# Attention and two MoEs on one core: the first MoE's weight conversions are cut into four parts, one place apart, and held in order

## The chip, the cores and the metric

The kernel runs on one core of a Trainium2 chip. The metric is the device time of one execution in microseconds, the median of three runs. Every time of an engine below comes from one profiled execution of the kernel before.

## The reference

All inputs are stored in 64 bits. The kernel works in 32-bit arithmetic on a high and a low part of each number, so a product of two numbers is three matmuls (high·high, high·low, low·high).

```
scores = q @ k^T / sqrt(64) + decay of log f, causal          (4 batches, 8 heads, 576 positions, 64 dims)
x  = softmax(scores) @ v                                      -> 2304 tokens x 512
h  = max(x @ w1, x @ w2, x @ w3)                              w1, w2, w3: 512 x 768
x2 = h @ w_out                                                w_out: 768 x 512
h2 = x2 @ w_in                                                w_in: 512 x 2048
g  = (a0 + a1 h2 + a2 h2^2 + a3 h2^3) / (1 + |b0| |h2| + |b1| h2^2 + 1e-6)
out = g @ moe2_w_out                                          moe2_w_out: 2048 x 512
```

## The kernel before

Attention is worked off in 20 pairs of heads (`pairs`), numbered 0 to 19. The first eight are batch 0, four for query group 0 and four for group 1 ("pair 8" is the first of batch 1). Tile names carry the numbers: `s3_0_8_1_1` is a bank of scores of pair 8, `e4_7_1_1` an exponential of pair 7, `tp`/`pt` the transposed exponentials, `o` the attention output, `x` its copy that the first MoE reads. TensorE also runs warm-up products (L84) at the start.

The first MoE takes 6 chunks of 128 hidden columns: `moe1_h(b, g, fc, j)` makes product j of chunk fc (tile `h0`, `h1` or `h2`; the running maximum is `m1`, `m2`), `moe1_o(b, g, dc)` the output `x2p`, copied to `xo`. These pieces of work are taken from a queue (`units`) and put between the attention's, six times per attention step (`fill`), so they fill TensorE while the attention waits. The output `x2p` needs all six chunks of `w_out` (`wo_0` to `wo_5`, each converted in two halves).

Weights come as 64-bit numbers and are converted on the chip in four parts (`stages`): the magnitude on ACT (L179, tile `cv_...`), four operations on its bits on DVE (L184, L185, L186, L189), the high part on ACT (L195), the low part by a subtraction on POOL (L198). The first MoE has 18 conversions of 128x512 (`cv_w0_0` to `cv_w2_5`, w1 to w3 of chunk 0 to 5) and 12 of 128x256 (`cv_wo_0_0` to `cv_wo_5_1`). `cv` tiles share six buffers with four live x tiles, so two conversions are under way at once: a magnitude waits for the low part of the conversion two before it. In `fill`, a conversion is one entry of the list `conv`: all four parts are issued in one place, with the load of the weights two conversions ahead in front (`pipelined`).

A scheduler puts the instructions of each engine into one static order, in which the engine then runs; a row waits for its inputs and everything behind it on that engine waits too. An instruction that is held (`keep_in_program_order`, here also `pinned`) stays behind the instruction of its engine that the program issued just before it; others are placed by the scheduler. Before, the conversions' parts are not held, and neither are the two operations on the gate's coefficients `ab` (L674 on DVE, L675 on ACT).

Of the kernel before, what the change touches and what calls it, by code (L numbers as in the profile page):

```python
# [11 lines left out]
AF = mybir.ActivationFunctionType  # L12
ALU = mybir.AluOpType
# [24 lines left out]
def kernel(  # L38
    ctx: ExitStack, tc: tile.TileContext, q, k, v, f, w1, w2, w3, w_out, m2_in, m2_out, m2_a, m2_b, out
):  # L40
    nc = tc.nc
# [6 lines left out]
    NF1 = FF1 // P  # L48
# [4 lines left out]
    def r32(ap):  # L53
        return ap.bitcast(F32)
# [7 lines left out]
    mpool = ctx.enter_context(tc.tile_pool(name="mpool", bufs=1, side="left"))  # L62
# [57 lines left out]
    LOOK, WHOLE, PRE = 2, 6, 2  # L120
# [33 lines left out]
    w1t, wot = {}, {}  # L154
# [6 lines left out]
    def load_raw(src, nm_):  # L161
        shape = list(src.shape)
        rp, rt, rb = (mpool, "x1", 8) if shape[1] * shape[2] <= 256 else (wpool, "x2", 6)
        raws[nm_] = rp.tile(shape[:-1] + [2 * shape[-1]], I32, name=f"raw_{nm_}", tag=rt, bufs=rb)
        tc.keep_in_program_order(nc.sync.dma_start(raws[nm_], src.bitcast(I32)))

    def stages(split, src, nm_, pool, tag, bufs, pin):
        shape = list(src.shape)
        at = {}

        def held(ins):
            return tc.keep_in_program_order(ins) if pin else ins

        def magnitude():
            raw = raws.pop(nm_)
            raw = raw.rearrange("p c (f t) -> p c f t", t=2)
            at["low"], at["top"] = raw[:, :, :, 0], raw[:, :, :, 1]
            at["t"] = pool.tile(shape, I32, name=f"cv_{nm_}", tag=tag, bufs=bufs)
            held(nc.scalar.activation(at["t"].bitcast(F32), at["top"].bitcast(F32), AF.Abs))  # L179

        def bits():
            t, low, top = at["t"], at["low"], at["top"]
            tf = t.bitcast(F32)
            held(nc.vector.tensor_scalar(tf, tf, E_LO, E_HI, op0=ALU.max, op1=ALU.min))  # L184
            nc.vector.tensor_scalar(t, t, 0x07FFFFFF, 3, op0=ALU.bitwise_and, op1=ALU.logical_shift_left)  # L185
            nc.vector.scalar_tensor_tensor(  # L186
                out=t, in0=low, scalar=29, in1=t, op0=ALU.logical_shift_right, op1=ALU.bitwise_or
            )
            nc.vector.scalar_tensor_tensor(  # L189
                out=t, in0=top, scalar=-0x40000000, in1=t, op0=ALU.bitwise_and, op1=ALU.bitwise_or  # L190
            )

        def high():
            at["hi"], at["lo"] = split()
            held(nc.scalar.activation(at["hi"], at["t"].bitcast(F32), AF.Copy))  # L195

        def low():
            held(nc.gpsimd.tensor_tensor(at["lo"], at["t"].bitcast(F32), r32(at["hi"]), op=ALU.subtract))  # L198

        return [magnitude, bits, high, low]  # L200

    def convert(hi, lo, src, nm_, pool, tag, bufs):
        for f_ in stages(lambda: (hi, lo), src, nm_, pool, tag, bufs, False):
            f_()

    def rows(w):
        return w.rearrange("(c p) f -> p c f", p=P)

    def raw_w1(fc, j):
        return rows((w1, w2, w3)[j])[:, :, fc * P : (fc + 1) * P], f"w{j}_{fc}"  # L210

    def convert_w1(fc, j):
        if fc not in w1t:
            w1t[fc] = [wpool.tile([P, 3, NDC, P], F32R, name=f"w1{x}_{fc}", tag="w", bufs=12) for x in "hl"]
        hi, lo = (t[:, j] for t in w1t[fc])
        convert(hi, lo, *raw_w1(fc, j), mpool, "x0", 6)

    def raw_wo(fc, z):
        return rows(w_out)[:, fc : fc + 1, z * 256 : (z + 1) * 256], f"wo_{fc}_{z}"

    def convert_wo(fc, z):
        if fc not in wot:
            wot[fc] = wpool.tile([P, 2, DM], F32R, name=f"wo_{fc}", tag="x2", bufs=6)
        hi, lo = (wot[fc][:, x : x + 1, z * 256 : (z + 1) * 256] for x in range(2))
        convert(hi, lo, *raw_wo(fc, z), mpool, "x0", 6)

    wpd = dram.tile([P, NF2, 2, DM], F32R, name="wpd")

# [18 lines left out]
    def pipelined(work, look):  # L247

        n = len(work)

        def go(i):
            for j in range(0 if i == 0 else i + look, min(i + look + 1, n)):
                work[j][0]()
            work[i][1]()

        return [lambda i=i: go(i) for i in range(n)]
# [5 lines left out]
    def pinned(ld):  # L262
        tc.keep_in_program_order(ld)
# [234 lines left out]
    def moe1_units(b, g):  # L498
# [7 lines left out]
    pairs = [Pair(n, *j) for n, j in enumerate(jobs)]  # L506
    slots = [Unit(p, h, g) for p in pairs for g in p.groups for h in range(2)]
    first = {u.pair.n: i for i, u in reversed(list(enumerate(slots)))}
    conv = [
        (lambda fc=fc, j=j: load_raw(*raw_w1(fc, j)), lambda fc=fc, j=j: convert_w1(fc, j))  # L510
        for fc in range(NF1)
        for j in range(3)
    ]
    conv += [
        (lambda fc=fc, z=z: load_raw(*raw_wo(fc, z)), lambda fc=fc, z=z: convert_wo(fc, z))
        for fc in range(NF1)
        for z in range(2)
    ]
    conv = pipelined(conv, LOOK)
    wps = [(c, z) for c in range(NF2) for z in range(2)]  # L520
    conv2 = []
    for i, cz in enumerate(wps):
# [19 lines left out]
    state = {"m": 0, "of": 1, "n": 0}  # L542
    queue = []

    def fill(step):

        want = conv_due(step)
        while conv and len(conv) > want:
            conv.pop(0)()
        if step >= CONV2[0] and conv2:  # L550
            state["c2"] += 4 * CONV2[1]
            while conv2 and state["c2"] >= 1:
                state["c2"] -= 1
                conv2.pop(0)()
        state["m"] += 1
        while units and (state["n"] - len(units)) * state["of"] < state["n"] * state["m"]:
            units.pop(0)()
        if not units and queue and queue[0][0] in ends:
            at, new = queue.pop(0)
            units.extend(new)  # L560
            state["of"] = max(1, NFILL * (ends[at] - step) - 3)
            state["n"], state["m"] = len(units), 0
# [2 lines left out]
    state["c"] = state["c2"] = 0.0  # L565

    def conv_due(step):
        state["c"] += 0.15 if step < 7 else 0.5
        return NCONV - int(state["c"])

    pairs[0].load()
# [8 lines left out]
    ab = const.tile([P, 8], F32, name="ab")  # L580
    pinned(nc.sync.dma_start(ab[:, 0:4], m2_a.partition_broadcast(P)))
    pinned(nc.sync.dma_start(ab[:, 4:6], m2_b.partition_broadcast(P)))
    for step in range(len(slots) + 2):
        u = slots[step] if step < len(slots) else None
        t = slots[step - 1] if 0 <= step - 1 < len(slots) else None
# [85 lines left out]
        for x in range(2):  # L671
            pinned(move(wpt[n][x][:, : c1 - c0], wpd[:, c0:c1, x]))

    nc.vector.tensor_scalar(ab[:, 0:4], ab[:, 0:4], -1.0, None, op0=ALU.mult)  # L674
    nc.scalar.activation(ab[:, 6:7], ab[:, 5:6], AF.Abs)  # L675
    nc.vector.memset(ab[:, 7:8], 1.0 + 1.0e-6)
    a0, a1, a2, a3, b0, _, b1, one = (ab[:, i : i + 1] for i in range(8))

# [160 lines left out]
```

## Time and profile before

| | |
|---|---|
| median of 3 runs | 963.07 us (962.58 to 964.19) |
| the profiled execution's own time | 963.76 us |
| its span on the core | 961.9 us, mean TensorE clock 0.991 |
| TensorE (PE) busy | 936.5 us, 97% |
| VectorE (DVE) busy | 728.7 us, 76% |
| ScalarE (ACT) busy | 642.7 us, 67% |
| GpSimd (POOL) busy | 254.7 us, 26% |

"Busy" counts a matmul from its issue to its modelled end, so PE shows as busy in a stretch in which it could do more; the number of its instructions in a window tells how much it did. [...]

### The profile page before, as it was taken

How to read it: one execution, taken by the hardware profiler on the slowest of the kernel's cores; microseconds unless marked ns; L12 is line 12 of the kernel's file. 1: busy time of each engine (PE TensorE's matmuls, PEld its weight loads, DVE VectorE, ACT ScalarE, POOL GpSimd, SP SyncE). 2: the span in 40 equal slices, each digit the busy share in tenths (PEclk: the TensorE clock that was granted, in tenths of full speed). 3: DMA queues.
4: the chain of work that ended last, by engine and by line, in shares of the span. 5: the costliest groups of instructions: out<-in, count | busy, mean ns of one | idle time of the engine just before them, and what ended most of it. 6: DMA issues, size and time to landing. Idle time of an engine off the chain costs nothing.

```text
span 961.9 us, 16831 instructions
## 1 busy us (share of the span) xinstructions
PE 936.5 (97%) x5780; PEld 828.1 (86%) x5780; DVE 728.7 (76%) x1689; ACT 642.7 (67%) x1526; POOL 254.7 (26%) x408
## 2 busy tenths in 40 slices
PE   7989989999999999999999999999999999999998
PEld 6758879997998999999999988888888888999997
DVE  4688985555776776535287969888988988899997
ACT  5886666777776777657444557667766766677765
POOL 2647664444553644524223400000000000000000
PEclk9988999999999999999999999999999999999999
DMA  5685323223455465230045567011002102100000
GB/s 154 165 241 142 81 56 102 54 55 106 130 144 186 134 176 154 70 100 7 27 151 175 165 238 287 1 45 44 1 1 66 44 1 64 46 1 1 33 1 33
DMA packets 125621, 88.52 MB, mean 92 GB/s; under 512 B 74448, under 2 KB 110304, under 8 KB 125536
## 3 DMA queue, kind: packets, MB, share of 16 engines
q1 hardware_dynamic: 125536, 87.45, 30.5%
q8 instruction: 46, 0.75, 0.3%
q14 instruction: 39, 0.32, 0.1%
HBM read 64.73 MB, written 22.69 MB: 91 GB/s over the span
## 4 chain that ended last, share of the span: by engine, by line
PE 79%; DVE 11%; ACT 4%; DMA 3%; issue 2%; POOL 0%; SPq 0%; DVEq 0%; ACTq 0%; POOLq 0%
PE hq L714 7%; PE hq L712 7%; PE oo L762 7%; PE hq L713 7%; PE oo L763 7%; PE oo L761 7%; PE h L465 5%; PE h L466 5%; PE h L467 5%; PE o L433 5%; PE tp L417 4%; PE s L380 2%; PE s L381 2%; PE x2p L490 2%; PE x2p L492 2%
## 5 line engine op out<-in xcount | busy, mean ns | idle before, releaser
L465 PE MATMUL h<-x,w1h 128*128 128x320 f32 (+1 forms) x576 | 176.9, 307 | 1.7 <-DVE x L441 1.1
L466 PE MATMUL h<-x,w1h 128*128 128x320 f32 (+1 forms) x576 | 172.8, 300 | 0.0
L467 PE MATMUL h<-x,w1l 128*128 128x320 f32 (+1 forms) x576 | 172.3, 300 | 0.0
L397 POOL TENSOR_SCALAR e<-e,rs 128x64 f32<-128x64 f32 (+4 forms) x160 | 89.4, 574 | 105.6 <-DVE rs L394 90.9
L388 ACT ACTIVATE e<-e,st 128x64 f32<-128x64 f32 (+4 forms) x160 | 89.1, 558 | 41.1 <-DVE st L382 39.8
L465 PEld LDWEIGHTS h<-x,w1h 128*128 128x128 f32 x576 | 109.8, 191 | 5.1 <-DVE x L441 2.0
L762 PE MATMUL oo<-wp,gh 128*128 128x512 f32 x288 | 112.6, 391 | 0.0
L761 PE MATMUL oo<-wp,gh 128*128 128x512 f32 x288 | 112.0, 389 | 0.0
L466 PEld LDWEIGHTS h<-x,w1h 128*128 128x128 f32 x576 | 110.0, 191 | 0.6 <-issue 0.5
L467 PEld LDWEIGHTS h<-x,w1l 128*128 128x128 f32 x576 | 109.8, 191 | 0.1
L721 ACT ACTIVATE s<-hq 128x512 f32<-128x512 f32 (+1 forms) x80 | 44.3, 554 | 97.7 <-PE hq L714 97.7
L763 PE MATMUL oo<-wp,gl 128*128 128x512 f32 x288 | 109.1, 391 | 0.0
L382 DVE CUSTOM_DVE_ANT_0 e<-s,mask 128x320 f32<-128x320 f32 (+3 forms) x160 | 67.6, 431 | 36.8 <-PE s L381 21.6
L419 ACT ACTIVATE pt<-tp 128x384 f32<-128x384 f32 (+3 forms) x160 | 69.6, 468 | 18.5 <-PE tp L417 15.6
L417 PE MATMUL tp<-ident,e 128*128 128x128 f32 (+1 forms) x480 | 77.9, 279 | 2.8 <-DVE k2s L310 1.7
L724 DVE SCALAR_TENSOR_TENSOR s<-s,ab,u 128x512 f32<-128x512 f32 (+1 forms) x80 | 55.7, 696 | 32.3 <-ACT u L722 32.1
L714 PE MATMUL hq<-x,wil 128*128 128x512 f32 (+1 forms) x192 | 69.9, 364 | 0.0
L712 PE MATMUL hq<-x,wih 128*128 128x512 f32 (+1 forms) x192 | 69.8, 363 | 0.0
L713 PE MATMUL hq<-x,wih 128*128 128x512 f32 (+1 forms) x192 | 69.7, 363 | 0.0
L763 PEld LDWEIGHTS oo<-wp,gl 128*128 128x128 f32 x288 | 54.1, 188 | 11.4
L761 PEld LDWEIGHTS oo<-wp,gh 128*128 128x128 f32 x288 | 54.1, 188 | 10.5
L417 PEld LDWEIGHTS tp<-ident,e 128*128 128x128 f32 (+1 forms) x480 | 55.8, 134 | 8.5 <-POOL e L397 2.7
(131 smaller groups left out, 2429.6 us busy)
## 6 DMA issues: line engine op xcount, KB each, us to landing
raw_w<-in_moe_w_dram SPq DMA_DIRECT2D x18, 512.0 KB
raw_wp<-in_moe_w_out_dram SPq DMA_DIRECT2D x32, 256.0 KB
wpd<-wp SPq DMA_DIRECT2D x32, 256.0 KB
raw_wi<-in_moe_w_in_dram SPq DMA_DIRECT2D x32, 256.0 KB
wp<-wpd SPq DMA_DIRECT2D x10, 768.0 KB
x2d<-xo SPq DMA_DIRECT2D x16, 320.0 KB
out_dram<-ob SPq DMA_DIRECT2D x18, 256.0 KB
kn<-in_k_dram SPq DMA_DIRECT2D x32, 128.0 KB
```

Of the source, the lines that this page charges most:

```text
L388: nc.scalar.activation(e[:nr], e[:nr], AF.Exp, bias=m, scale=-1.0, accum_out=l)
L397: nc.gpsimd.tensor_scalar(e, e, self.rs[:, 1, j : j + 1], 0.0, op0=ALU.mult, op1=ALU.add)
L417: nc.tensor.transpose(tp[:kr, dst : dst + P], self.e[i][:, Q0[c] : Q1[c]], ident)
L465: nc.tensor.matmul(hp_[:, :w], wh[:, j, dc], xs[dc][:, 1], start=(dc == NDC - 1), stop=False)
L466: nc.tensor.matmul(hp_[:, :w], wh[:, j, dc], xs[dc][:, 0], start=False, stop=False)
L467: nc.tensor.matmul(hp_[:, :w], wl[:, j, dc], xs[dc][:, 0], start=False, stop=(dc == 0))
L712: nc.tensor.matmul(hp_[:, :w], wih[:, dc, fs], xh, start=(dc == 0), stop=False)
L713: nc.tensor.matmul(hp_[:, :w], wih[:, dc, fs], xl, start=False, stop=False)
L714: nc.tensor.matmul(hp_[:, :w], wil[:, dc, fs], xh, start=False, stop=(dc == NDC - 1))
L761: nc.tensor.matmul(o, g[0][:, ts_], wh_, start=(fc == 0), stop=False)
L762: nc.tensor.matmul(o, g[0][:, ts_], wl_, start=False, stop=False)
L763: nc.tensor.matmul(o, g[1][:, ts_], wh_, start=False, stop=(fc == NF2 - 1))
```

## The change

Each of the 30 conversions becomes two entries of `conv`, an even and an odd place. Even place k loads the weights two ahead, issues the high part of conversion k−1 and then the magnitude of conversion k. Odd place k issues the low part of conversion k−1 and then the bits of conversion k. All of these are held on their engine (of the four DVE operations the first). The pace doubles, since there are twice as many entries: as many conversions per step as before, each ending one place later. L674 and L675 are held too, which keeps them behind the instructions issued before them at the end of the attention.

```diff
-    conv = [
-        (lambda fc=fc, j=j: load_raw(*raw_w1(fc, j)), lambda fc=fc, j=j: convert_w1(fc, j))
...
-    conv = pipelined(conv, LOOK)
+    firsts = [(raw_w1(fc, j), lambda fc=fc, j=j: split_w1(fc, j)) for fc in range(NF1) for j in range(3)]
+    firsts += [(raw_wo(fc, z), lambda fc=fc, z=z: split_wo(fc, z)) for fc in range(NF1) for z in range(2)]
+    parts1 = [stages(split, *raw, mpool, "x0", 6, True) for raw, split in firsts]
+
+    def part1(i, *which):
+        if 0 <= i < len(parts1):
+            for x in which:
+                parts1[i][x]()
+
+    def even(k):
+        for raw, _ in firsts[0 if k == 0 else k + LOOK : k + LOOK + 1]:
+            load_raw(*raw)
+        part1(k - 1, 2)
+        part1(k, 0)
+
+    def odd(k):
+        part1(k - 1, 3)
+        part1(k, 1)
+
+    conv = []
+    for i in range(len(firsts) + 1):
+        conv += [lambda i=i: even(i), lambda i=i: odd(i)]
...
-        state["c"] += 0.15 if step < 7 else 0.5
+        state["c"] += 0.3 if step < 7 else 1.0
...
-    nc.vector.tensor_scalar(ab[:, 0:4], ab[:, 0:4], -1.0, None, op0=ALU.mult)
-    nc.scalar.activation(ab[:, 6:7], ab[:, 5:6], AF.Abs)
+    pinned(nc.vector.tensor_scalar(ab[:, 0:4], ab[:, 0:4], -1.0, None, op0=ALU.mult))
+    pinned(nc.scalar.activation(ab[:, 6:7], ab[:, 5:6], AF.Abs))
```

The change adds and removes no instruction of an engine that computes; it moves them. Line numbers from about L210 on differ between the two kernels: from the pairs to the first MoE's products those of the changed kernel are lower by two (L382 there reads L380, L490 reads L488). The text uses those of the kernel before.

On DVE, around the conversion of chunk 4 (the number at the end of a name counts tiles), the order before is:

```order
L184 TENSOR_SCALAR cv_w0_4_861<-cv_w0_4_861 128x512
L185 TENSOR_SCALAR cv_w0_4_861<-cv_w0_4_861 128x512
L186 SCALAR_TENSOR_TENSOR cv_w0_4_861<-raw_w0_4_795,cv_w0_4_861 128x512
L184 TENSOR_SCALAR cv_w1_4_902<-cv_w1_4_902 128x512
L189 SCALAR_TENSOR_TENSOR cv_w0_4_861<-raw_w0_4_795,cv_w0_4_861 128x512
L394 RECIPROCAL rs_5_1_1_1116<-rs_5_1_1_1116 128x2
L185 TENSOR_SCALAR cv_w1_4_902<-cv_w1_4_902 128x512
L186 SCALAR_TENSOR_TENSOR cv_w1_4_902<-raw_w1_4_818,cv_w1_4_902 128x512
```

and in the changed kernel:

```order
L184 TENSOR_SCALAR cv_w0_4_852<-cv_w0_4_852 128x512
L185 TENSOR_SCALAR cv_w0_4_852<-cv_w0_4_852 128x512
L186 SCALAR_TENSOR_TENSOR cv_w0_4_852<-raw_w0_4_771,cv_w0_4_852 128x512
L189 SCALAR_TENSOR_TENSOR cv_w0_4_852<-raw_w0_4_771,cv_w0_4_852 128x512
L439 TENSOR_TENSOR x_4_1_1_1044<-o_4_1_1_1033,x_4_1_1_1044 128x256
L184 TENSOR_SCALAR cv_w1_4_894<-cv_w1_4_894 128x512
L185 TENSOR_SCALAR cv_w1_4_894<-cv_w1_4_894 128x512
```

Two conversions were woven into each other; now the four rows of one stand together, and the next conversion's first follows its last with one other row between.

On ACT, at the same conversions, the order before is:

```order
L179 ACTIVATE cv_w0_4_861<-raw_w0_4_795 128x512
L135 ACTIVATE q2s01_1635<-mask_92,unit_99 2x320
L388 ACTIVATE e4_5_1_1_1132,rs_5_1_1_1116<-e4_5_1_1_1132,st_5_1_1_1115 128x576
L179 ACTIVATE cv_w1_4_902<-raw_w1_4_818 128x512
L393 ACTIVATE rs_5_1_1_1116<-rs_5_1_1_1116,tiny_97 128x2
L470 ACTIVATE m0_0_0_0_882<-h0_0_0_0_869 128x320
L195 ACTIVATE w1h_4_859<-cv_w0_4_861 128x512
```

and in the changed kernel:

```order
L179 ACTIVATE cv_w0_4_852<-raw_w0_4_771 128x512
L417 ACTIVATE pt1_128<-tp0_5_0_1_1067 128x512
L438 ACTIVATE x_4_1_1_1044<-o_4_1_1_1033 128x256
L417 ACTIVATE pt1_128<-tp1_5_0_1_1078 128x384
L195 ACTIVATE w1h_4_891<-cv_w0_4_852 128x512
L179 ACTIVATE cv_w1_4_894<-raw_w1_4_811 128x512
```

The magnitude of `w1_4` stood ahead of the high part of `w0_4`; now it stands right behind it.

On DVE, at the end of the conversions, the order before is:

```order
L189 SCALAR_TENSOR_TENSOR cv_wo_5_0_1496<-raw_wo_5_0_1417,cv_wo_5_0_1496 128x256
L189 SCALAR_TENSOR_TENSOR cv_wo_5_1_1514<-raw_wo_5_1_1450,cv_wo_5_1_1514 128x256
L382 ISA e4_7_1_1_1599,st_7_1_1_1591<-s4_1_7_1_1_1604,mask_92,st_7_1_1_1591 128x256
L382 ISA st_7_1_1_1591 128x1
L394 RECIPROCAL rs_7_1_1_1592<-rs_7_1_1_1592 128x2
L495 TENSOR_TENSOR xo_0_0_0_2072<-x2p_0_0_0_2053,xo_0_0_0_2072 128x320
```

and in the changed kernel:

```order
L380 ISA e4_8_0_1_1859,st_8_0_1_1851<-s4_1_8_0_1_1864,mask_92,st_8_0_1_1851 128x256
L380 ISA st_8_0_1_1851 128x1
L184 TENSOR_SCALAR cv_wo_5_1_1513<-cv_wo_5_1_1513 128x256
L185 TENSOR_SCALAR cv_wo_5_1_1513<-cv_wo_5_1_1513 128x256
L380 ISA e3_8_1_1_1942,st_8_1_1_1940<-s3_0_8_1_1_1943,mask_92 128x448
L380 ISA st_8_1_1_1940 128x1
L186 SCALAR_TENSOR_TENSOR cv_wo_5_1_1513<-raw_wo_5_1_1441,cv_wo_5_1_1513 128x256
...
L189 SCALAR_TENSOR_TENSOR cv_wo_5_1_1513<-raw_wo_5_1_1441,cv_wo_5_1_1513 128x256
```

Before, the last conversion and `xo_0_0_0` behind it stand among the rows of pair 7. In the changed kernel both stand among those of pair 8: 25 rows, nearly all of pair 8's attention, are ahead of `xo_0_0_0` that were behind it (12 scores rows at L382, each with its small read-out row, 5 at L310, 4 at L322, 3 reciprocals and an x). Ahead of that, the scores come earlier among the conversions: the four bits operations of 20 conversions stood ahead of pair 6's last scores row on DVE, and 16 do now. PE's order answers to it: 53 matmuls of pair 8's attention stand ahead of the first product with `wo_5` that stood behind it, 71 ahead of `x2p_0_0_2`; at `h0_1_0_0` (batch 1's first product) less than ten are left of that, and the second MoE's rows on PE are in the same order in both kernels. L674 and L675 stand just ahead of the second MoE's first gate instead of at the 13th microsecond.

## Rows read from the trace of the kernel before

**Rows 1.** The page, chain that ended last, shares of the span.

```profile
PE 79%; DVE 11%; ACT 4%; DMA 3%; issue 2%; POOL 0%; SPq 0%; DVEq 0%; ACTq 0%; POOLq 0%
```

**Rows 2.** Windows (us, busy us of each engine (instructions), TensorE clock, DMA share, GB/s).

```profile
10.00:20.00 10.00, 9.06 (x49) 7.06 (x48) 2.48 (x17) 6.18 (x22) 1.24 (x4) 1.00 0.47 114
70.00:80.00 10.00, 8.74 (x27) 6.16 (x27) 9.89 (x21) 7.47 (x18) 7.91 (x7) 0.50 0.61 194
160.00:170.00 10.00, 10.00 (x88) 9.27 (x85) 6.66 (x21) 7.11 (x19) 7.47 (x14) 1.00 0.30 68
220.00:230.00 10.00, 8.54 (x65) 5.90 (x64) 5.77 (x23) 8.32 (x27) 4.07 (x9) 1.00 0.59 168
```

**Rows 3.** The same view, one window over the conversions' stretch.

```profile
52.00:142.00 90.00, 80.19 (x483) 65.84 (x480) 80.95 (x182) 61.33 (x152) 53.47 (x61) 0.91 0.47 130
```

**Rows 4.** The same window, instructions on tile cv_w alone.

```profile
52.00:142.00 90.00, 36.03 (x48) 14.97 (x24) 17.81 (x12) 0.91 0.47 130
```

**Rows 5.** The same window, instructions on tile cv_wo alone.

```profile
52.00:142.00 90.00, 23.44 (x48) 10.00 (x24) 9.70 (x12) 0.91 0.47 130
```

**Rows 6.** Line L184, 10 to 52 us (ns min/median/max).

```profile
L184 DVE TENSOR_SCALAR cv_w<-cv_w x6: 406/424/428, 22.5 to 40.1; 128x512 f32<-128x512 f32 x6
```

**Rows 7.** Line L186, 10 to 52 us.

```profile
L186 DVE SCALAR_TENSOR_TENSOR cv_w<-raw_w,cv_w x6: 676/690/932, 23.4 to 42.6; 128x512 int32<-128x512 int32 x6
```

**Rows 8.** Line L184, 52 to 142 us.

```profile
L184 DVE TENSOR_SCALAR cv_wo<-cv_wo x12: 278/291/1006, 103.6 to 132.1; 128x256 f32<-128x256 f32 x12
```

**Rows 9.** Line L186, 52 to 142 us.

```profile
L186 DVE SCALAR_TENSOR_TENSOR cv_wo<-raw_wo,cv_wo x12: 407/517/1445, 104.5 to 135.9; 128x256 int32<-128x256 int32 x12
```

**Rows 10.** Line L198, 52 to 142 us.

```profile
L198 POOL TENSOR_TENSOR w1l<-cv_w,w1h x12: 1273/1447/1716, 59.7 to 104.4; 128x512 fp32r<-128x512 f32 x12
L198 POOL TENSOR_TENSOR wo<-cv_wo,wo x12: 731/814/957, 108.8 to 139.2; 128x256 fp32r<-128x256 f32 x12
```

**Rows 11.** Groups by line and form, 52:142: busy us, mean ns | idle before, releaser.

```profile
L179 ACT ACTIVATE cv_w<-raw_w 128x512 f32<-128x512 f32 x12 | 7.9, 667 | 3.4 <-DMA raw_w<-in_moe_w_dram 2.2 <-POOL w1l L198 1.2
...
L195 ACT ACTIVATE w1h<-cv_w 128x512 fp32r<-128x512 f32 x12 | 7.5, 627 | 6.1 <-DVE cv_w L189 6.1
L184 DVE TENSOR_SCALAR cv_w<-cv_w 128x512 f32<-128x512 f32 x12 | 7.4, 617 | 2.5 <-ACT cv_w L179 2.3
...
L179 ACT ACTIVATE cv_wo<-raw_wo 128x256 f32<-128x256 f32 x12 | 5.1, 436 | 1.5 <-POOL wo L198 0.8 <-POOL w1l L198 0.6
L195 ACT ACTIVATE wo<-cv_wo 128x256 fp32r<-128x256 f32 x12 | 5.0, 414 | 5.1 <-DVE cv_wo L189 4.9
L382 DVE CUSTOM_DVE_ANT_0 e<-s,mask 128x448 f32<-128x448 f32 x8 | 4.9, 616 | 0.1
...
L184 DVE TENSOR_SCALAR cv_wo<-cv_wo 128x256 f32<-128x256 f32 x12 | 4.7, 395 | 1.3 <-ACT cv_wo L179 1.2
```

**Rows 12.** Timeline of DVE (start us, us).

```profile
64.73 0.85 DVE L185 TENSOR_SCALAR cv_w<-cv_w 128x512 int32<-128x512 int32 x1
65.62 1.64 DVE L186 SCALAR_TENSOR_TENSOR cv_w<-raw_w,cv_w 128x512 int32<-128x512 int32 x1
67.18 0.41 DVE L184 TENSOR_SCALAR cv_w<-cv_w 128x512 f32<-128x512 f32 x1
```

**Rows 13.** Timeline of POOL, the same stretch.

```profile
65.27 1.44 POOL L198 TENSOR_TENSOR w1l<-cv_w,w1h 128x512 fp32r<-128x512 f32 x1
```

**Rows 14.** Timeline of POOL, ACT and DVE at one hand-over.

```profile
82.97 2.97 POOL L198 TENSOR_TENSOR w1l<-cv_w,w1h 128x512 fp32r<-128x512 f32 x2
83.58 0.63 ACT L195 ACTIVATE w1h<-cv_w 128x512 fp32r<-128x512 f32 x1 [1.97 <-DVE cv_w L189]
...
84.71 0.67 ACT L179 ACTIVATE cv_w<-raw_w 128x512 f32<-128x512 f32 x1 [0.51 <-POOL w1l L198]
...
85.41 0.81 DVE L184 TENSOR_SCALAR cv_w<-cv_w 128x512 f32<-128x512 f32 x1 [1.87 <-ACT cv_w L179]
```

**Rows 15.** The chain from 10 to 24 us (start us, us, what).

```profile
12.61 3.40 DMA ab<-in_moe_b_dram
```

More of the change, by code (lines that the diff above doesn't have):

```diff
@@ L210, in raw_w1, with split_w1, split_wo @@
         return rows((w1, w2, w3)[j])[:, :, fc * P : (fc + 1) * P], f"w{j}_{fc}"
-    def convert_w1(fc, j):
+    def split_w1(fc, j):
         if fc not in w1t:
             w1t[fc] = [wpool.tile([P, 3, NDC, P], F32R, name=f"w1{x}_{fc}", tag="w", bufs=12) for x in "hl"]
-        hi, lo = (t[:, j] for t in w1t[fc])
-        convert(hi, lo, *raw_w1(fc, j), mpool, "x0", 6)
+        return [t[:, j] for t in w1t[fc]]
     def raw_wo(fc, z):
         return rows(w_out)[:, fc : fc + 1, z * 256 : (z + 1) * 256], f"wo_{fc}_{z}"
-    def convert_wo(fc, z):
+    def split_wo(fc, z):
         if fc not in wot:
             wot[fc] = wpool.tile([P, 2, DM], F32R, name=f"wo_{fc}", tag="x2", bufs=6)
-        hi, lo = (wot[fc][:, x : x + 1, z * 256 : (z + 1) * 256] for x in range(2))
-        convert(hi, lo, *raw_wo(fc, z), mpool, "x0", 6)
+        return [wot[fc][:, x : x + 1, z * 256 : (z + 1) * 256] for x in range(2)]
     wpd = dram.tile([P, NF2, 2, DM], F32R, name="wpd")
@@ L508 @@
     first = {u.pair.n: i for i, u in reversed(list(enumerate(slots)))}
-    conv = [
-        (lambda fc=fc, j=j: load_raw(*raw_w1(fc, j)), lambda fc=fc, j=j: convert_w1(fc, j))
[L511 to L518, printed above, removed]
-    conv = pipelined(conv, LOOK)
+    firsts = [(raw_w1(fc, j), lambda fc=fc, j=j: split_w1(fc, j)) for fc in range(NF1) for j in range(3)]
[16 more added lines that the diff above has]
+        conv += [lambda i=i: even(i), lambda i=i: odd(i)]
     wps = [(c, z) for c in range(NF2) for z in range(2)]
```

## The prediction

> **What bounds the kernel now.** The chain that ended last comes first: 79% of the span is TensorE (PE) and 11% VectorE (DVE) [rows 1]. The windows say where the DVE part lies. In 160:170 PE issues 88 matmuls in 10 us, 0.114 us each, and is full [rows 2]. In 52:142, where 24 of the first MoE's 30 conversions run, it issues only 483 in 90 us, while DVE is busy 80.95 of the 90 [rows 3]. So here DVE sets the pace and PE waits for what it makes. Two windows of the tiles show what DVE does: 36.03 us on `cv_w` (48 operations, 12 conversions, 3.00 us each) and 23.44 on `cv_wo` (1.95 each) [rows 4, 5]. Behind this stretch PE is nearly always full, so what is lost in it stays lost; the one hole after it that concerns us is 220:230, with 65 matmuls [rows 2].
>
> **DVE's price for a conversion is not its own.** Undisturbed, L184 takes 0.424 us and L186 0.690 [rows 6, 7], and L185 and L189 go like these; a `cv_w` conversion is then 2 × (0.424 + 0.690) = 2.23 us. For `cv_wo` I take 0.29 and, as the shortest of its scan operations, 0.41 [rows 8, 9], so 1.40. Over the window that is 12 × 2.23 + 12 × 1.40 = 43.6 us against 59.5 measured: 15.9 us are stretching. The timeline shows the cause: L186 at 65.62 takes 1.64 us, to 67.26 [rows 12], and POOL's low part ran from 65.27 to 66.71 [rows 13]. The DVE operation ends 0.55 us after the low part does. It did not run slower beside it, it hardly ran.
>
> **The change, part by part,** against the profiled execution's 963.76 us, which is 0.7 above the median.
>
> (a) Order of the work. 25 rows of DVE work, mostly pair 8's, now lie ahead of the first MoE's output. By the forms' means in the stretch (0.616 us for the largest L382 [rows 11], a reciprocal about 0.16) I estimate 10.2 us, and 9.5 when neighbours overlap as at 67.18, which starts 0.08 before the row ahead of it ends [rows 12]. Against it PE gets 71 matmuls to do ahead of `x2p_0_0_2`: 71 × 0.114 = 8.1 us. What PE loses by waiting longer for the last conversion, it does meanwhile: +9.5 − 8.1 = **+1.4**. Bounds: −8.1, if DVE is not what PE waits for there, and +9.5, if PE waited elsewhere for lack of the work moved.
>
> (b) Hand-over waits. Since ACT runs in order and the magnitude of k now stands behind the high part of k−1, DVE's L184 of k waits after L189 of k−1 for L195 and L179: 0.627 + 0.667 = 1.29 us for `cv_w`, 0.414 + 0.436 = 0.85 for `cv_wo` [rows 11], less the rows that stand between on DVE. The order has 24 such places in the stretch. In two of the twelve of `cv_w` nothing stands between, in nine a row or a few short ones, in one enough: I get 10.5 us of waits. For `cv_wo` four have nothing between, four some, four enough: 5.0 us. Before, DVE waited there 2.5 + 1.3 = 3.8 us [rows 11]. So 15.5 − 3.8 = **+11.7**. The trace shows the hand-over once: L195 at 83.58, L179 at 84.71 (0.51 of it waiting for a low part), L184 at 85.41, with DVE idle 1.87 us [rows 14]. Bounds: 0, if DVE is not the bound at these places; 24 × 1.3 = 31 as the trace's worst kind.
>
> (c) Less stretching. The low part of k−1 can start when its high part is done, beside the magnitude of k, so it now runs in the wait. It takes at least 1.273 us for `cv_w` and 0.731 for `cv_wo` [rows 10], the magnitude 0.667 and 0.436, so it outlasts the wait by 0.61 or 0.30 us. L184 would be caught in this rest, as at 85.41, where it took 0.81 us and the low parts ended at 85.94 (82.97 + 2.97) [rows 14]. So the 15.9 us of stretching fall to about 11 × 0.6 + 9 × 0.3 = 9.3: **−6.6**. Bounds: −15.9, if L184 runs freely beside a low part, and 0.
>
> [...]
>
> (d) Dependent neighbours. The four bits operations now stand in a row, and each needs the one before: L186 at 65.62 starts 0.04 after L185's end, where independent rows overlap by 0.08 [rows 12]. Some 15 more such pairs at 0.12: **+1.8**.
>
> (e) ACT's own work. The high part is needed at once now, but waits behind whatever stands ahead of it on ACT, which is busy 61.33 of the 90 us [rows 3]. 20 places at 0.08: **+1.5** (0 to +5). Behind it, magnitude, L184 and so DVE are late too.
>
> (f) The ab operations. L675 leaves the start, where its DMA stands in the chain with 3.40 us [rows 15]. But PE is busy 9.06 of 10 us in 10:20, with its warm-up products [rows 2], so it gains only its holes: **−1.0** (0 to −2.8). At the new place, the DMA is long done and PE full: nothing, hidden by the products queued there.
>
> (g) Loads. Loading raw weights earlier takes away ACT's wait for `raw_w`, 2.2 us in the stretch [rows 11]. Half of it I count: **−1.2** (0 to −2.2). The loads now stand ahead of kn_2 on the DMA queue; PE has its warm-up products to cover a late kn_2, without which it would cost what three loads take.
>
> (h) The hole in 220:230. There the first MoE's pieces have run out; now they come some 8 us later and fill it: (88 − 65) × 0.114 = 2.6 us missing, of which I take **−2.0** (0 to −2.6).
>
> Parts that only change place in the second MoE have the same order on PE and cost nothing, since PE is full there.
>
> Sum: 1.4 + 11.7 − 6.6 + 1.8 + 1.5 − 1.0 − 1.2 − 2.0 = +5.6. One correction: DVE's other waits in the stretch. It is idle 90 − 80.95 = 9.05 us, of which 3.8 are counted in (b). The other 5.2 are for PE and ACT, and partly vanish when DVE runs late: **−2.2** (0 to −5). That leaves +3.4: 967.2 for the profiled execution, **966.5** for the median.
>
> **Rivals.** [...]
>
> *Faster, about 957.* The waits of (b) fall where PE has attention work: 16 conversions stand ahead of pair 6's last scores on DVE where 20 did, four of some 3 us or less each, so PE is fed some 10 us earlier from 70:80 on, where it is poorest. Then (b) costs only half, 5.8, and the sum is 3.4 − 5.9 = −2.5; with (c) at −11 it is −6.9, thus 956.2. It decides when half of the hand-overs lie behind a PE that has work. For it: 27 matmuls in 70:80 leave much to win. Against it: DVE is at 9.89 of 10 there [rows 2], and it has the 9.5 us of (a) more to do before `x2p` can go on.
>
> *No change, 963.* Everything in the stretch is an exchange: (b) and (c) cancel, PE's work ahead covers (a), and the pieces that are late come even by batch 1. It needs (b) to be 3 us less, well within its bounds.
>
> **How the numbers follow.** What a measurement of this kernel tells from no change is about 0.2%, 1.9 us. The forecast case (964.9 to 969) has 0.35, the slower rival 0.18, no change 0.20, faster 0.27: together faster 0.27, same 0.20, slower 0.53. The range runs from 957, at the faster rival, to 973, the slower one and a little of what (e) can still add; what lies outside has about 2 in 10.
>
> **What would show it.** After the change, DVE's idle time before L184 in the first MoE's stretch should be near 15 us and be released by L179, against 3.8; L186 and L189 should come down to near 0.69 us, and L184 go up; a `cv_w` conversion should fall from 3.00 us on DVE to about 2.8. `xo_0_0_0` should come some 10 us later than before, the scores of pair 8 earlier. L675 should no longer stop ACT near 13 us, and 220:230 should hold over 80 matmuls. The prediction is wrong if those waits are there but PE's matmuls in 52:142 do not fall, or if the order of the loads makes a new wait for kn_2 or for a raw weight.

## The result, and the profile after

The changed kernel takes 969.71 us in the median (967.89 to 973.23, 5 runs) against 963.07 before (also 5 runs); the ratio is 1.0075 with a 95% interval of 1.0063 to 1.0087. The change makes the kernel slower by about 7 us. The runs spread over 5 us where those of before spread over 1.6; the longest also has the lowest mean TensorE clock (0.977, against 0.983 to 0.985 in the other four). The profiled execution is the shortest of the five: 967.89 us, 4.1 above that of before.

On the page of the changed kernel, DVE has a smaller share of the chain that ended last (8% for 11%) and PE a larger one:

```profile
PE 84%; DVE 8%; ACT 4%; issue 2%; DMA 1%; SPq 0%; POOL 0%; DVEq 0%; ACTq 0%; POOLq 0%
```

This row alone would mislead. PE's share also holds matmuls at a granted clock of 0.50 (19 in 75:85). The windows of the changed kernel show where the time went (columns as in [rows 2]):

```profile
10.00:20.00 10.00, 9.80 (x54) 7.81 (x52) 3.97 (x20) 7.34 (x25) 1.68 (x4) 1.00 0.63 183
70.00:80.00 10.00, 4.95 (x19) 2.91 (x17) 7.94 (x16) 6.02 (x15) 5.42 (x6) 0.67 0.30 92
80.00:90.00 10.00, 7.15 (x39) 5.28 (x40) 6.44 (x11) 5.53 (x12) 3.00 (x3) 0.62 0.58 188
140.00:150.00 10.00, 5.97 (x29) 4.82 (x29) 8.13 (x23) 7.08 (x21) 7.34 (x12) 0.78 0.18 46
220.00:230.00 10.00, 10.00 (x86) 9.02 (x86) 3.38 (x13) 5.69 (x20) 3.15 (x7) 1.00 0.14 34
...
52.00:142.00 90.00, 74.07 (x449) 60.79 (x447) 72.74 (x159) 54.66 (x137) 44.65 (x53) 0.89 0.47 131
```

In 52:142 PE issues 449 matmuls, 34 fewer than before, and DVE is busy 8 us less [rows 3]: DVE did not become faster, it waits. Two poor stretches stand out, 70:90 and 140:150. The hole in 220:230 has closed (86 matmuls for 65 [rows 2]) and 10:20 holds 54 for 49.

What DVE waits for is one line. The waits of DVE in 52:162 of the changed kernel (us in total, times, longest), and below them the same two of the kernel before:

```profile
DVE cv_w L184 <- ACT cv_w L179: 11.1, 11, 1.4
DVE cv_wo L184 <- ACT cv_wo L179: 4.3, 7, 0.8
...
DVE cv_w L184 <- ACT cv_w L179: 2.3, 2, 1.9
DVE cv_wo L184 <- ACT cv_wo L179: 1.2, 2, 0.9
```

15.4 us against 3.5 before. The waits of PE in the same stretch show who pays. The x of L439 (L441 before) and the maximum m of L470 (L472 before) stand on DVE behind conversions; POOL's L395 (L397 before) follows a reciprocal on DVE. The changed kernel, and below it the two of these waits that the kernel before has:

```profile
PE tp L415 <- POOL e L395: 6.9, 3, 2.6
PE o L431 <- DVE x L439: 5.0, 1, 5.0
PE h L463 <- DVE m L470: 2.8, 2, 2.3
...
PE h L465 <- DVE m L472: 0.7, 2, 0.4
PE tp L417 <- POOL e L397: 0.6, 1, 0.6
```

One hand-over, in the timelines of DVE, ACT and POOL of the changed kernel:

```profile
56.75 0.69 DVE L189 SCALAR_TENSOR_TENSOR cv_w<-raw_w,cv_w 128x512 int32<-128x512 int32 x1
...
58.70 1.04 DVE L184 TENSOR_SCALAR cv_w<-cv_w 128x512 f32<-128x512 f32 x1 [0.86 <-ACT cv_w L179]
...
57.47 0.63 ACT L195 ACTIVATE w1h<-cv_w 128x512 fp32r<-128x512 f32 x1 [0.48 <-DVE cv_w L189]
58.01 0.66 ACT L179 ACTIVATE cv_w<-raw_w 128x512 f32<-128x512 f32 x1
...
58.18 1.27 POOL L198 TENSOR_TENSOR w1l<-cv_w,w1h 128x512 fp32r<-128x512 f32 x1 [3.65 <-ACT w1h L195]
```

L189 ends at 57.44. Then come the high part, the magnitude, and only at 58.70 the next L184; a scores row on DVE covers some of the wait, 0.86 us is idle. The low part runs from 58.18 to 59.45, and L184, undisturbed 0.42 us long, ends at 59.74, 0.29 us after it.

The groups of the conversions in 52:162 of the changed kernel (busy us, mean ns | idle before, releaser):

```profile
L184 DVE TENSOR_SCALAR cv_w<-cv_w 128x512 f32<-128x512 f32 x12 | 11.7, 975 | 11.1 <-ACT cv_w L179 11.1
L186 DVE SCALAR_TENSOR_TENSOR cv_w<-raw_w,cv_w 128x512 int32<-128x512 int32 x12 | 9.3, 779 | 0.2
L189 DVE SCALAR_TENSOR_TENSOR cv_w<-raw_w,cv_w 128x512 int32<-128x512 int32 x12 | 9.0, 754 | 0.2
...
L185 DVE TENSOR_SCALAR cv_w<-cv_w 128x512 int32<-128x512 int32 x12 | 7.9, 658 | 0.2
L184 DVE TENSOR_SCALAR cv_wo<-cv_wo 128x256 f32<-128x256 f32 x12 | 7.6, 637 | 4.3 <-ACT cv_wo L179 4.3
```

Last, when the same matmul starts in both profiled executions (the static order of PE set against the trace; us):

```
                                  before   after
first of h0_0_0_0                  76.86   86.88   +10.0
last scores bank of pair 7        132.73  139.29    +6.6
x2p_0_0_2                         142.33  164.06   +21.7
last scores bank of pair 8        160.95  161.60    +0.7
h0_1_0_0, where the orders meet   231.09  239.30    +8.2
last scores bank of pair 15       353.07  358.73    +5.7
first product of the second MoE   562.93  567.16    +4.2
```

The loss is made between 52 and 165 us. Pair 8, whose attention was drawn ahead, ends on time, while the first MoE's output is 22 us late. 8.2 us are left where the two orders meet, and some 4 of them are given back in holes that before had further on.

### The profile page after: what moved, and what is told of

Same layout as the page of the kernel before. It is cut to its first block, busy times and chain, and to the rows that moved or that the text cites. A ratio compares the mean times of both kernels' runs of the same rounds, so it can differ in the third digit from the quotient of the medians.

```text
span 966.1 us, 16847 instructions
## 1 busy us (share of the span) xinstructions
PE 936.7 (97%) x5780; PEld 829.2 (86%) x5780; DVE 731.0 (76%) x1689; ACT 641.2 (66%) x1526; POOL 250.2 (26%) x408
## 4 chain that ended last, share of the span: by engine, by line
PE 84%; DVE 8%; ACT 4%; issue 2%; DMA 1%; SPq 0%; POOL 0%; DVEq 0%; ACTq 0%; POOLq 0%
PE hq L724 7%; PE oo L772 7%; PE hq L723 7%; PE hq L722 7%; PE oo L773 7%; PE oo L771 7%; PE h L463 6%; PE h L464 6%; PE h L465 6%; PE o L431 5%; PE tp L415 5%; PE x2p L488 2%; PE x2p L489 2%; PE x2p L490 2%; PE s L379 2%
## 5 line engine op out<-in xcount | busy, mean ns | idle before, releaser
L395 POOL TENSOR_SCALAR e<-e,rs 128x64 f32<-128x64 f32 (+4 forms) x160 | 88.3, 566 | 115.2 <-DVE rs L392 88.5
L380 DVE CUSTOM_DVE_ANT_0 e<-s,mask 128x320 f32<-128x320 f32 (+3 forms) x160 | 67.2, 432 | 31.7 <-PE s L379 19.5
L415 PE MATMUL tp<-ident,e 128*128 128x128 f32 (+1 forms) x480 | 80.7, 286 | 7.2 <-POOL e L395 6.9
L431 PE MATMUL o<-pt,v 128*64 128x256 f32 (+2 forms) x512 | 59.1, 374 | 5.6 <-DVE x L439 5.0
```

What stands on the lines that cost most here:

```text
L415: nc.tensor.transpose(tp[:kr, dst : dst + P], self.e[i][:, Q0[c] : Q1[c]], ident)
L431: mm = nc.tensor.matmul(ot[SIDES[i][0], q0 - lo : w], p.v[:, c, i], p.pt[g][:, i, col : col + hi - q0], start=(j == 0), stop=(j == len(ord ...
```

## The experiments

Each kernel is compared with the kernel before on the same chip. The table has its median, the ratio with its 95% interval, and the difference in us that follows from the ratio:

```
                                                   median    ratio (interval)            us
e1_ab      ab operations held, nothing else        962.26   0.9986 (0.9977 to 0.9994)   -1.4
e2_conv    conversions changed, ab as before       969.41   1.0060 (1.0047 to 1.0074)   +5.8
changed    both                                    969.71   1.0075 (1.0063 to 1.0087)   +7.2
e3_swap    magnitude k ahead of high k-1           963.28   0.9996 (0.9987 to 1.0005)   -0.4
e4_free    cut, not held                           960.69   0.9965 (0.9953 to 0.9978)   -3.4
e5_whole   not cut, held                           958.67   0.9950 (0.9937 to 0.9962)   -4.8
e9_pace    changed, conversions earlier            976.51   1.0132 (1.0116 to 1.0147)  +12.7
e10_late   e3_swap, conversions later              966.20   1.0030 (1.0018 to 1.0042)   +2.9
e6_after_fill   changed, low parts not computed    962.38   0.9986 (0.9977 to 0.9995)   -1.3
e7_before_fill  before, low parts not computed     950.29   0.9863 (0.9849 to 0.9877)  -13.2
e8_warm    e9_pace with more warm-up products      983.90   1.0222 (1.0207 to 1.0238)  +21.4
e11_halves e4_free, low parts in two halves        956.89   0.9932 (0.9919 to 0.9944)   -6.6
e12_whole_halves  e5_whole, low parts in halves    963.04   0.9993 (0.9984 to 1.0002)   -0.7
```

**Which part of the change?** e1_ab holds L674 and L675 in the kernel before, and nothing else; e2_conv is the changed kernel without that.

```diff
-    nc.scalar.activation(ab[:, 6:7], ab[:, 5:6], AF.Abs)
+    pinned(nc.scalar.activation(ab[:, 6:7], ab[:, 5:6], AF.Abs))
```

> The kernel before with only the two ab operations held. Theory (hand-over of the conversions): the loss is not here; ScalarE no longer waits 2.8 us near 13 us and the scores behind come about 2 us earlier, but TensorE has warm-up products there, so 961 to 963.2. Rival (the ab operations cost at their new place, ahead of the first gate): 965 or more, and a hole in TensorE near 563 us.

> The changed kernel with the ab operations as before, so the conversions' part alone. Theory (hand-over): 969 to 972, with some 15 us of DVE idle before L184 released by L179 in the first MoE's stretch, as in the changed kernel. Rival (the ab operations carry the loss): 963 to 965.

The loss is the conversions' part; in e2_conv DVE waits 15.7 us before L184. The ab part alone gains 1.4 us: with L675 gone from ACT's start, PE runs 2.1 us earlier through the first MoE's stretch, and 1.7 us at the end. On top of the changed conversions this gain cannot be seen (+5.8 without it, +7.2 with it, in a kernel whose runs spread over 5 us), though of the two profiled executions the one with it is 2.3 us shorter (967.89 for 970.22); why the medians do not show it stays open.

**Is it the order on ACT, the cut or the hold?** e3_swap exchanges two calls:

```diff
     def even(k):
...
-        part1(k - 1, 2)
-        part1(k, 0)
+        part1(k, 0)
+        part1(k - 1, 2)
```

> The changed kernel with the two calls of the even place swapped: the magnitude of k ahead of the high part of k-1, all still held and cut into two places. Theory (hand-over): DVE's idle before L184 falls from 15.4 us to under 4, no matmul-poor window near 145 us, 961 to 965. Rival (the cut itself, a conversion that ends one place later and two entries, or the hold costs): the waits go but the time stays at 968 or more.

e4_free gives `stages` False in place of True, so the parts are cut but not held:

> The changed kernel with the conversions cut as there, but not held. In its order only 5 of 29 magnitudes stand behind the high part of the conversion ahead (29 in the changed kernel). Theory (hand-over, made by the hold): DVE's idle before L184 under 5 us, 962 to 965. Rival (the cut and its pace cost, not the hold): 968 or more.

e5_whole leaves the conversions whole, in one place, and holds all their parts:

```diff
-        convert(hi, lo, *raw_w1(fc, j), mpool, "x0", 6)
+        convert(hi, lo, *raw_w1(fc, j), mpool, "x0", 6, True)
```

> The kernel before, its conversions still whole in one place, but all their parts held (and the ab operations held too, which alone was worth -1.4). In its order 9 of 29 magnitudes stand behind the high part ahead (8 before, 29 in the changed kernel), with some 4 us of waits by the rows. Theory (it is the order high part before magnitude that costs, not the hold): 961 to 964. Rival (holding the parts costs in itself): 966 or more.

The same two rows of DVE's waits in 52:162 of e3_swap:

```profile
DVE cv_w L184 <- ACT cv_w L179: 0.7, 2, 0.4
DVE cv_wo L184 <- ACT cv_wo L179: 0.6, 2, 0.4
```

15.4 us of waits become 1.3, and the whole loss is gone, with the cut and the hold in place. So neither of the two costs in itself; it is the high part ahead of the magnitude that does. But the swap moves more than the waits: 21 conversions stand ahead of pair 6's last scores row on DVE in e3_swap, where 16 do in the changed kernel and 20 before, so the late order of the work is gone with them. Not held, or held and whole, the kernel is even faster than expected (e4_free 960.69, below the 962 given; e5_whole 958.67, below the 961 given). In e5_whole scores of pair 4 come up to 5.0 us earlier on PE than before and the clock in 52:162 is 0.95 for 0.92; what in its order earns the rest beyond the 1.4 of the ab part is not settled.

**Waits, or the order of the work?** In the changed kernel two things go together: the hand-over waits, and attention drawn ahead of the conversions. A change of pace separates them. e9_pace keeps the waits and draws the conversions forward; e10_late has no such waits and puts the conversions about as late as the changed kernel does (0.75 entries per fill, on e3_swap).

```diff
-        state["c"] += 0.3 if step < 7 else 1.0
+        state["c"] += 0.3 if step < 7 else 1.3
```

> The changed kernel with a quicker pace of its conversions (1.3 entries per fill in place of 1.0 from step 7 on). Every magnitude still stands behind the high part ahead of it, but the order of the work is again like before: 23 conversions ahead of pair 6's last scores on DVE (16 in the changed kernel, 20 before), 14 matmuls of pair 8 ahead of x2p_0_0_2 (52 in the changed kernel, 8 before, by the names with an 8). Theory (the hand-over waits cost): still some 15 us or more of DVE idle before L184, 968 to 973. Rival (the order of work costs: late conversions behind attention): 962 to 965.

> The kernel e3_swap (magnitude ahead of the high part, held) with a slower pace, 0.75 entries per fill. No hand-over of the kind, but the order of work of the changed kernel: 18 conversions ahead of pair 6's last scores, 56 matmuls of pair 8 ahead of x2p_0_0_2. Theory (hand-over waits cost): DVE idle before L184 under 4 us, 962 to 966. Rival (the order of work costs): 968 to 972, with x2p_0_0_2 some 20 us later than before.

```
                           conversions early      conversions late
without hand-over waits    e3_swap   963.3        e10_late  966.2
with hand-over waits       e9_pace   976.5        changed   969.7
```

With the waits, early conversions cost 13 us more than without, late ones 3.5. Late conversions alone cost 2.9 of the 7.2 us. So the waits are the larger part of the loss and the late order of the work, which comes with them, the smaller one. That the attention drawn ahead softens the waits, because it stands between the conversions and fills DVE's and PE's time, is a reading of the table and not shown by itself. The table is not a clean two by two: 23 conversions stand ahead of pair 6's last scores row in e9_pace and 21 in e3_swap, 16 in the changed kernel and 18 in e10_late, and e3_swap at the pace of e9_pace was not run. But both of the rival's expectations fail: with early conversions the waits should have cost nothing. The theory's own ranges were missed too, by 3.5 us in e9_pace (976.5 for 973 at most), whose clock in 52:162 is down to 0.83, and by 0.2 in e10_late. The waits of DVE in 52:162 of e9_pace are as in the changed kernel, and more:

```profile
DVE cv_w L184 <- ACT cv_w L179: 9.3, 9, 1.3
DVE cv_wo L184 <- ACT cv_wo L179: 7.6, 9, 1.2
```

**What is the blocking by POOL worth?** In e6_after_fill and e7_before_fill POOL fills the first MoE's low parts with zeros and reads nothing:

```diff
+            if nm_[:2] in ("w0", "w1", "w2", "wo"):
+                held(nc.gpsimd.memset(r32(at["lo"]), 0.0))
+                return
```

> The changed kernel with the first MoE's low parts left out: POOL fills them with zeros (a write that reads nothing) in place of the subtraction, so the product misses the weights' low parts. If the low part's reads block DVE, L184 falls from 0.98 to near 0.43 us and a cv_w conversion from 3.17 to about 2.3 us on DVE, while the hand-over waits stay near 15 us: 963 to 967. Rival (the stretching of DVE's operations comes from something else, or does not lie on the path): 968 or more.

> The kernel before with the first MoE's low parts filled with zeros in the same way. If the blocking is what stretches DVE there, cv_w falls from 3.00 to about 2.3 us, 14 to 16 us of DVE time go, and the time falls by 4 to 9 us, to 954 to 959. Rival (not on the path): within 1 us of before.

DVE on `cv_w` and `cv_wo`, windows of the tiles, e7_before_fill in 52:172 (columns as in [rows 4], without POOL's, which no longer reads these tiles):

```profile
52.00:172.00 120.00, 29.97 (x48) 15.09 (x24) 0.96 0.46 125
...
52.00:172.00 120.00, 19.88 (x48) 9.99 (x24) 0.96 0.46 125
```

and e6_after_fill:

```profile
52.00:172.00 120.00, 30.23 (x48) 14.28 (x25) 0.89 0.45 123
...
52.00:172.00 120.00, 20.76 (x48) 8.95 (x24) 0.89 0.45 123
```

Against 36.03 + 23.44 = 59.5 us before [rows 4, 5], DVE takes 49.9 us when a fill that reads nothing stands in the low part's place: 9.6 us of the 15.9 of stretching go. The trace of e7_before_fill shows where the other 6.3 lie. Of the 96 operations, the 53 that stand beside no POOL instruction took their undisturbed times to within 0.02 us. Of the other 43, 30 stand beside other POOL work (L400, L481, L314, L328) and are together 3.8 us too long; 13 stand beside a fill and are 5.0 us too long, all of it in L184 and L185 or beside other POOL work as well. (These are the operations' own times; neighbours overlap, so they come to more than 6.3.) So the fill is not harmless, and 9.6 us is probably less than what the low part costs. Two places in that trace, each with the DVE row and the fills beside it:

```profile
86.20 1.21 DVE L185 TENSOR_SCALAR cv_w<-cv_w 128x512 int32<-128x512 int32 x1
85.67 1.46 POOL L199 MEMSET w1l<- 128x512 f32 x3
...
78.12 0.69 DVE L186 SCALAR_TENSOR_TENSOR cv_w<-raw_w,cv_w 128x512 int32<-128x512 int32 x1
77.75 1.74 POOL L199 MEMSET w1l<- 128x512 f32 x3
```

L185 ends 0.28 us after the last fill; L186 takes no longer than undisturbed.

Taking the 9.6 us away gains 13.2, more than itself. Not all of the 13.2 need be blocking: the fill is also shorter than the subtraction (0.57 us for 1.49 in the mean on 128x512), and ACT's waits for a low part, 2.6 us in the kernel before, are gone with it. In the changed kernel the same step makes 37.99 + 23.04 = 61.0 (the same view and window) into 51.0, and gains 8.5. In both kernels, then, the subtraction, set against the fill, is worth nearly 10 us of DVE's busy time (9.6 and 10.0); the change moved this and did not lessen it. In the kernel's time it is worth 13.2 us before and 8.5 in the changed kernel. And without it the changed kernel is 12 us slower than the kernel before (962.4 against 950.3), so it is not the blocking that makes the order expensive. Both kernels came out faster than expected (below 963 and below 954), though less DVE time went than the 14 to 16 us given.

**Does the clock carry the loss?** e8_warm gives the banks of pairs 4 to 6 in e9_pace the same warm-up products as the first four.

```diff
-        if n < 4:
+        if n < 7:
```

> The kernel e9_pace with the warm-up products of line 84 also for pairs 4 to 6 (96 more, some 20 us of TensorE work, which add nothing to the result). It tests the clock: e9_pace has a granted clock of 0.83 in 52:142. If the fallen clock makes up much of the loss, the clock comes to 0.95 or more there and the time falls, to 968 to 974. If the loss is DVE's waits alone, the clock rises and the time stays within 2 us of 976.5; if TensorE has no room for the products, it rises to 980 and more.

The windows of e8_warm in 52:162 and, second, of e9_pace:

```profile
52.00:162.00 110.00, 97.85 (x591) 82.02 (x588) 87.61 (x188) 63.67 (x161) 52.23 (x65) 0.97 0.40 110
```

```profile
52.00:162.00 110.00, 90.63 (x527) 73.81 (x525) 87.30 (x199) 65.86 (x168) 52.79 (x69) 0.83 0.43 119
```

The clock stays up (0.97 for 0.83) and the time still rises, by some 8 us. The products were not free, so this bounds little: it shows that the clock was not worth more than their cost in place, and how many of the 7 us of the change are the clock's stays open.

**A version that beats both.** L184 at 58.70 of the changed kernel took 1.04 us for 0.42 and ended 0.29 us after the low part beside it. If an operation caught like this waits for the end of the POOL instruction, which one place does not show, shorter POOL instructions should hold it up for less time. e11_halves takes e4_free and does each low part in two halves:

```diff
+                n = shape[-1] // 2
+                for part in (slice(0, n), slice(n, None)):
+                    nc.gpsimd.tensor_tensor(lo[:, :, part], t[:, :, part], r32(hi[:, :, part]), op=ALU.subtract)
```

> The kernel e4_free with each low part of the first MoE done by POOL in two halves. If a DVE operation that is caught waits for the end of the POOL instruction that is running, L186 and L189 are caught for half as long where they come once per low part: their means fall by 0.1 us or more and the time to 957 to 960. Rival (a caught operation is caught by either half in turn, and POOL's own time grows by some 0.2 us per half): 960.5 to 964.

Three groups of e4_free in 52:162, and then the same of e11_halves:

```profile
L186 DVE SCALAR_TENSOR_TENSOR cv_w<-raw_w,cv_w 128x512 int32<-128x512 int32 x12 | 12.6, 1049 | 0.2
L189 DVE SCALAR_TENSOR_TENSOR cv_w<-raw_w,cv_w 128x512 int32<-128x512 int32 x12 | 9.5, 793 | 0.1
L185 DVE TENSOR_SCALAR cv_w<-cv_w 128x512 int32<-128x512 int32 x12 | 9.4, 782 | 0.2
```

```profile
L186 DVE SCALAR_TENSOR_TENSOR cv_w<-raw_w,cv_w 128x512 int32<-128x512 int32 x12 | 10.9, 910 | 0.2
L189 DVE SCALAR_TENSOR_TENSOR cv_w<-raw_w,cv_w 128x512 int32<-128x512 int32 x12 | 9.8, 815 | 0.1
...
L185 DVE TENSOR_SCALAR cv_w<-cv_w 128x512 int32<-128x512 int32 x12 | 6.1, 510 | 0.2
```

It is the fastest that computes everything, 956.89 us, 0.9932 of before, though POOL's own time for a low part of `cv_w` grows from 1.42 us to twice 0.94. The expectation holds in part. L186 and L185 of `cv_w` come down, L189 does not, and on `cv_wo` L186 and L189 go up (0.55 to 0.60 us, 0.50 to 0.57), as the rival had it. DVE's busy time on the two tiles falls by some 3 us in all. Added to e5_whole, where these halves are held as well, the same step does not gain but loses:

> The two gains together: e5_whole (conversions whole, parts held, -5.0) with each low part in two halves (worth 3.8 on e4_free). If the hold's gain and the shorter blocking are of different kinds they add up in part: 954 to 957. Rival (both take the same idle time of TensorE in the first MoE's stretch): 957 to 960, no better than e11_halves at 956.9.

DVE's waits before L184 in e12_whole_halves (10:172) are

```profile
DVE cv_w L184 <- ACT cv_w L179: 6.7, 8, 2.7
DVE cv_wo L184 <- ACT cv_wo L179: 0.6, 2, 0.4
```

against 5.4 in e5_whole. That is too little to explain 4 us. The trace shows one more thing that grew: in 52:162 ACT's magnitudes wait 12.0 us for low parts on POOL, for 3.4 in e5_whole. But in e11_halves they wait 13.4, and that kernel is fast. The order differs from e5_whole's in many other places, and the cause was not found.

## Why the prediction was right, and where it was not

The direction and the mechanism of the waits were right; the profiled execution came at 967.9 where the sum had 967.2, the median at 969.7 where 966.5 was given, within the range. That the sum came so near is in part luck: step (c) failed as it was described, and a return that the sum did not have made up for part of it.

(b) Hand-over waits: 15.5 us predicted, 15.4 measured, at the places and with the releaser named. e3_swap and e10_late show that this is the larger part of the loss.

(c) Less stretching: predicted −6.6, measured +1.5 (61.0 us on the two tiles for 59.5). This is the step that failed. Of the +1.5, 2.3 us are overlap of neighbouring rows that is gone, which belongs to (d) (+1.8 there): the 96 operations' own times add up to 61.8 us before and 61.0 in the changed kernel, so that stretching fell by 0.8. The step put all of the stretching down to the low part, from two rows beside which a low part ran, and let L184 alone be caught afterwards. What L184 catches came nearly as predicted: 12 × (0.975 − 0.424) + 12 × (0.637 − 0.291) = 10.8 us for 9.3. What it left out is the rest. L186 and L189 of `cv_w`, at 0.93 and 0.96 us before, came only to 0.78 and 0.75 instead of 0.69: none of them stands beside a low part any more, but nine stand beside other POOL work and make all of the excess. L185 rose from 0.60 us to 0.66 instead of coming to 0.42: three of the twelve are caught by a low part. The prediction's bound of 0 for this term was the right end in DVE's time. In the kernel's time e6_after_fill and e7_before_fill say something else: the subtraction, set against the fill, costs 4.7 us less in the changed kernel than before (8.5 for 13.2), and the order without it costs 11.9 us, where the sum without (c) has 10.0. Why a like amount of blocking costs the kernel less there, no run shows.

(a) The exchange of +1.4: `x2p_0_0_2` is 21.7 us late, and `xo_0_0_0` 21 where some 10 were foreseen; the scores of pair 8 end 0.7 us later than before and not earlier. e10_late puts the price of the late order at 2.9 us.

(f) The ab operations: −1.0 predicted, −1.4 measured alone. (h) The hole in 220:230 closed, 86 matmuls for "over 80". Beyond that, PE's lag falls by another 2.7 us between pairs 13 and 15, in a hole of before that the sum did not have (56 matmuls in 290:300, 73 in the changed kernel). With this return the profiled execution comes near the sum: at `h0_1_0_0` the loss was 8.2 us, with the ab gain in it. (e) and (g) were not measured by themselves.

The slower rival's time came up in single runs (971.45 and 973.23 us). The clock, at 0.50 in 75:85, fell again later (0.78 in 140:150, 1.00 in that window before); what that is worth was not separated. The faster rival had the wrong sign. That attention ahead of the conversions makes good a part of the waits is possible (e9_pace, without it, is at 976.5), but not shown.

That a DVE operation beside a low part hardly runs until the low part ends was read from single places (L186 at 65.62, ending 0.55 us after it [rows 12, 13], and in the changed kernel L184 at 58.70, 0.29 us after it); why the one holds up the other, no run shows.

## What to carry to other kernels

When work goes round several in-order engines (ACT, DVE, ACT, POOL), look at the pair of instructions that meet on the engine visited twice. Putting the last part of one piece ahead of the first part of the next turns two pieces under way into one, and the engine between waits for both (DVE 15.4 us before L184, 1.3 with the two swapped); swapping two lines was worth 6 to 8 us here (963.28 us for 969.71). An instruction that is stretched should be priced by taking its neighbour away and by looking at every row with its neighbours, not by the one row in which the neighbour is seen to stretch it. And shorter POOL instructions are worth a try where DVE is the bound: halving the low parts gained 3 us in e4_free, but lost 4 in e5_whole.

## What the runs showed of the hardware

With a fill in place of POOL's subtractions 9.6 us of DVE time went, and 13.2 us of the kernel; how much of the difference comes from the fill's reading nothing and how much from its being shorter (0.57 us for 1.49) was not tried. POOL took longer for a low part of `cv_w` in two halves (1.88 us for 1.42) and e4_free was still 3 us faster with them. Of the 96 operations of the conversions on DVE in e7_before_fill, the 53 that stood beside no POOL instruction took their undisturbed times to within 0.02 us. Beside a POOL fill, which only writes, they differed: the L186 at 78.12 took no longer than undisturbed (0.69 us), while the L185 at 86.20 took 1.21 us for 0.42.
